# Retention followed by a squared-ReLU feed-forward: Strassen in eight groups for the first product, a scaled cast, a plain eviction and a new order

## The chip, the cores and the metric

The kernel runs on one core of a Trainium2 chip. The metric is the device time of one execution in microseconds (us). All inputs lie in the chip's memory in fp32, the output goes back there in fp32; in between the kernel works in fp16 with fp32 sums.

## The reference

```python
# q, k, v: [8 batch, 8 heads, 576 positions, 64]
scores = (q @ k^T) / sqrt(64)
ret    = scores * Dmat            # Dmat[h,i,j] = gamma_h ** (i-j) for i >= j, else 0
x      = (ret @ v) -> [4608 tokens, 512]        # heads side by side
h      = x @ w_in                               # w_in [512, 2048]
g      = relu(h) ** 2
out    = g @ w_out                              # w_out [2048, 512], out [4608, 512]
```

There are 4608 tokens. Most of the multiplications lie in the two products with `w_in` and `w_out`; the rest is the retention (a linear attention whose mask decays by a factor gamma to the distance, one gamma for each head).

## The kernel before

**Units and groups.** The 4608 tokens are cut into 36 units of 128 tokens. Of these, 32 are "full" units (128 positions of one batch) and 4 are "tails" (the last 64 positions of two batches). Two units make a group; there are 18 groups. The weights stay in SBUF as fp16, and a group passes through two stages.

**Retention of a group** (`add_casts`, `add_ret`). SyncE's queue loads q, k and v of a unit (256 KB each, L438 to L444). GpSimd casts them: k by a copy (L516), q by a copy (L527), v by a multiplication with a decay vector (L532). The cast k and q of the first eight units are transposed by TensorE (L584); for the other 28 units a DMA transposes them (tile `kqT`, L543). TensorE then works in small multiplications of 64x64 (all at L502): `psc` are the scores, `psS` the state of k and v that the next position block needs, `psO` the result. VectorE multiplies the scores by the mask (L838, tile `rT`), makes the decayed state (`Rm` L859, `stmp` L863, `R` L611) and multiplies the result by gamma to the position on the way out of PSUM (L898, tile `xT`). These 64x64 multiplications stand in dense blocks: the `psO` and `psc` of several units one after another. `PADS` (L202) says how many empty instructions the recorder sets between other multiplications ahead of each block.

**Feed-forward of a group** (`add_ff`). First product: for each pair of 128 columns of `w_in`, 4 multiplications of 128x256 for each half (L1229) fill a PSUM bank `ph`; ScalarE takes the relu into a tile `rl` (L1237), and ScalarE (L1247) or VectorE (L1249) squares it into `gT`. That is 64 multiplications of 128x256 for a group. Second product: group 0 in the plain way (L1270, 128x512), groups 1 to 17 by Strassen's method in the form of Winograd (`add_strassen`, L1327): seven products of half the size in each dimension instead of eight, from sums that VectorE makes (L1300, tile `gS`), and joined behind TensorE by copies on ScalarE (L1340) and additions on VectorE (L1350).

**Strassen for the first product** (`add_ff1s`) is used in groups 14, 15 and 16 (`FSET`). VectorE makes four small differences of `xT` (L1057). Each half j of the output columns takes seven products of 8 multiplications of 128x128 (L1072), so a group takes 112 of them. ScalarE copies three of the seven out of PSUM (L1085), VectorE adds two such parts and takes the relu (L1106), ScalarE takes the plain relu of one (L1100) and squares 1024 columns at a time (L1120). The four sums of weights that this needs (L1032, tile `wS`) are made by VectorE once; they wait for `xT` of groups 4 and on.

**What sets the order.** Every instruction is added to a recorder with an engine, dependences and the buffers that it takes and gives back. A planner (`emit`, L107) simulates the engines with fixed durations and takes the ready task with the lowest key; the keys stand in a list of 1794 numbers, `PLACES` (L20). Instructions are then issued in the order of that simulation, and each engine works in its own order, waiting on semaphores. In `add_ff1s` and `add_strassen` each product also depends on the one before it in the same group. The weights come in eight transfers of 512 KB on GpSimd's DMA queue (L478): four for `w_in`, then four for `w_out`.

Of the kernel before, what the change touches and what calls it, by code (L numbers as in the profile page):

```python
# [16 lines left out]
RESERVE_FROM = 200.0  # L17


PLACES = """  # L20
# [55 lines left out]
""".split()  # L76


# [1392 lines left out]
```

## Time and profile before

| what | value |
|---|---|
| runs (3) | 284.87, 284.90, 284.92 us; median 284.9 |
| span of the profiled execution | 284.5 us |
| lies around the span, against the median | 0.4 us |
| TensorE granted clock | full speed in every slice |
| TensorE busy | 277.1 us in 4490 instructions |
| VectorE busy | 195.8 us in 371 instructions |
| ScalarE busy | 190.6 us in 360 instructions |
| GpSimd busy | 87.3 us in 123 instructions |
| DMA | 50.0 MB, mean 176 GB/s |
| L1229, first product, plain | 960 multiplications of 128x256, 117.4 us busy |
| L1072, first product, Strassen | 336 multiplications of 128x128 |
| L898, `xT` out of PSUM | 28 of 683 ns on VectorE |
| L527, q's cast | 24 of 700 ns in the mean, on GpSimd |

Busy time is the time in which an engine's records cover the span. A multiplication's record is longer than its share of TensorE's time, since records overlap: a 128x256 record is 273 ns, but 40 of them take 4.37 us. So the cost of a multiplication is read from start to start in a run of equal ones, and not from the record. "DVE" is VectorE, "ACT" ScalarE, "POOL" GpSimd, "SP" SyncE, "PE" TensorE. A row of waits says which instruction waited, for whom, for how long in total, how often, and the longest.

### The profile page before, as it was taken

To read this page: it belongs to the slowest core of one execution; us is meant where nothing else is said; L and a number is where in the kernel's file an instruction comes from. 1 tells how busy PE (TensorE), PEld (TensorE's weight loads), DVE (VectorE), ACT (ScalarE), POOL (GpSimd) and SP (SyncE) were. 2 spreads that over 40 slices of the span, in tenths; PEclk is the share of its full clock that TensorE was granted. 3 is DMA by queue.
4 is the path that set the end of the run, shared out by engine and by line. 5 is a ranking of instruction groups with operands and counts; after the bars stand their busy time and mean duration, and the time that the engine had idled before them with its cause. 6 is when DMAs were issued, how large, how long until landed. Compare 5 with 4: busy or idle time off the path is not lost.

```text
span 284.5 us, 10916 instructions
## 1 busy us (share of the span) xinstructions
PE 277.1 (97%) x4490; PEld 237.7 (84%) x4490; DVE 195.8 (69%) x371; ACT 190.6 (67%) x360; POOL 87.3 (31%) x123
## 2 busy tenths in 40 slices
PE   8899999999999999899999999999999999999994
PEld 3578767888888888788888888888988999899883
DVE  4783489756867769635859485866986889765742
ACT  5659884678495848566575767577657486668830
POOL 6550035445334346434342523353243200000000
PEclk9999999999999999999999999999999999999999
DMA  7999998999997989999989969999998902020205
GB/s 204 291 207 205 261 313 233 155 241 167 197 189 165 225 193 177 195 241 198 234 196 215 208 163 198 200 146 249 200 168 215 193 0 78 2 76 1 76 0 150
DMA packets 119152, 50.00 MB, mean 176 GB/s; under 512 B 94784, under 2 KB 113728, under 8 KB 119104
## 3 DMA queue, kind: packets, MB, share of 16 engines
q1 hardware_dynamic: 114560, 44.84, 73.4%
q0 software_dynamic: 4224, 4.19, 8.9%
q8 instruction: 37, 0.61, 0.9%
q10 hardware_dynamic: 320, 0.26, 0.3%
q14 instruction: 11, 0.09, 0.1%
HBM read 36.70 MB, written 9.44 MB: 162 GB/s over the span
## 4 chain that ended last, share of the span: by engine, by line
PE 84%; DMA 11%; SPq 3%; POOL 1%; issue 0%; DVE 0%; POOLq 0%
PE po L1327 36%; PE ph L1229 31%; PE ph L1072 7%; DMA w_out<-in_moe_w_out_dram 6%; PE psO L502 4%; DMA pair<-in_v_dram 2%; PE po L1270 2%; PE psc L502 2%; PE psS L502 2%; DMA kqT<-kq 2%; SPq L460 1%; DMA loads<-in_v_dram 1%; SPq L463 1%; PE psT L584 1%; POOL w_out L478 1%; SPq L543 0%
## 5 line engine op out<-in xcount | busy, mean ns | idle before, releaser
L1229 PE MATMUL ph<-xT,w_in 128*128 128x256 f16 x960 | 117.4, 273 | 0.0
L1229 PEld LDWEIGHTS <-w_in 128*128 128x128 f16 x960 | 93.3, 98 | 11.8
L1237 ACT ACTIVATE rl<-ph 128x512 f16<-128x512 f32 x120 | 70.4, 590 | 42.3 <-PE ph L1229 41.7
L1247 ACT ACTIVATE gT<-rl 128x512 f16<-128x512 f16 x101 | 63.4, 630 | 2.7
L1327 PEld LDWEIGHTS <-gS 128*128 128x128 f16 x544 | 51.6, 98 | 6.1
L1327 PE MATMUL po<-wT,gS 128*128 128x256 f16 x408 | 54.9, 273 | 0.0
L1327 PEld LDWEIGHTS <-gT 128*128 128x128 f16 x408 | 39.5, 98 | 4.8
L1300 DVE TENSOR_TENSOR gS<-gT,gS 128x512 f16<-128x512 f16 (+1 forms) x51 | 32.3, 640 | 9.9 <-ACT gT L1247 9.2
L532 POOL TENSOR_TENSOR v<-loads,vdec_full 128x512 f16<-128x512 f32 x24 | 27.2, 1133 | 36.1 <-DMA loads<-in_v_dram 33.0
L1327 PE MATMUL po<-w_out,gT 128*128 128x256 f16 x272 | 37.6, 273 | 0.0
L1300 DVE TENSOR_TENSOR gS<-gT 128x1024 f16<-128x1024 f16 x34 | 25.7, 760 | 11.8 <-ACT gT L1247 9.0
L516 POOL CAST kq<-loads 128x512 f16<-128x512 f32 x32 | 22.1, 692 | 34.7 <-DMA loads<-in_k_dram 26.9
L1350 DVE TENSOR_TENSOR o<-po,u 128x256 f32<-128x256 f32 x33 | 13.9, 422 | 22.7 <-PE po L1327 14.6
L527 POOL CAST kq<-loads 128x512 f16<-128x512 f32 x24 | 16.8, 700 | 31.0 <-DMA loads<-in_q_dram 31.0
L1340 ACT COPY u<-po 128x256 f32<-128x256 f32 x34 | 12.4, 368 | 16.6 <-PE po L1327 16.4
L898 DVE TENSOR_TENSOR xT<-psO,gam_full 128x512 f16<-128x512 f32 x28 | 18.6, 683 | 5.8 <-PE psO L502 5.7
L1327 PE MATMUL po<-wT,gT 128*128 128x256 f16 x136 | 18.8, 273 | 0.0
L1327 PE MATMUL po<-w_out,gS 128*128 128x256 f16 x136 | 18.6, 273 | 0.0
L838 DVE TENSOR_TENSOR rT<-psc,mask_full 128x512 f16<-128x512 f32 x24 | 15.7, 681 | 0.6 <-PE psc L502 0.6
L1106 DVE CUSTOM_DVE_ANT_0 gT<-ph,loads 128x512 f16<-128x512 f32 x18 | 12.1, 685 | 4.2 <-PE ph L1072 3.5
L611 DVE TENSOR_TENSOR R<-stmp,dec 128x512 f16<-128x512 f32 (+1 forms) x18 | 13.5, 750 | 0.4
L1350 DVE TENSOR_TENSOR o<-po,p 128x256 f32<-128x256 f32 x18 | 7.6, 422 | 7.2 <-issue 3.5
(101 smaller groups left out, 310.3 us busy)
## 6 DMA issues: line engine op xcount, KB each, us to landing
out_dram<-o SPq DMA_DIRECT2D x32, 256.0 KB, 2.8
loads<-in_k_dram SPq DMA_DIRECT2D x24, 256.0 KB, 4.6
loads<-in_q_dram SPq DMA_DIRECT2D x96, 64.0 KB, 3.1
loads<-in_v_dram SPq DMA_DIRECT2D x24, 256.0 KB, 3.8
w_in<-in_moe_w_in_dram POOLq DMA_DIRECT2D x4, 512.0 KB, 8.9
w_out<-in_moe_w_out_dram POOLq DMA_DIRECT2D x4, 512.0 KB, 14.4
pair_c<-in_k_dram SPq DMA_DIRECT2D x2, 512.0 KB
pair_c<-in_q_dram SPq DMA_DIRECT2D x4, 256.0 KB
```

The costliest lines, as they stand in the source:

```text
L502: t = nc.tensor.matmul(out_, lhsT=lhsT, rhs=rhs, start=start, stop=True, skip_group_check=True, tile_position=(64 * row, 64 * col))
L516: op(out=out_.rearrange("p (n b a d) -> p n b a d", n=2, b=2, a=2), in_=in_.rearrange("p (a n b) d -> p n b a d", n=2, a=2))
L527: nc.gpsimd.tensor_copy(out=tile_of["kq", u][:, 1].rearrange("p (t a d) -> p a t d", t=4, a=2), in_=tile_of["q32", u].rearrange("p (a t) d ...
L532: nc.gpsimd.tensor_tensor(out=t, in0=tile_of["v32", u], in1=vdec[kind].rearrange("p (h o) -> p h o", o=1).to_broadcast([P, H, D]), op=ALU. ...
L898: nc.vector.tensor_tensor(out=tile_of["x", g].rearrange("p n (s e i) -> p e (n s) i", s=n, e=2)[:, c], in0=y.rearrange("p (o t r) -> p o r ...
L1072: nc.tensor.matmul(out_[:, e], lhsT=left[:, m, fi * P:(fi + 1) * P], rhs=right()[:, m], start=fresh and e == 0 and m == 0, stop=m == HK - ...
L1229: nc.tensor.matmul(tile_of["ph", g, fb][:, j, :], lhsT=w_in16[:, m, fi * P:(fi + 1) * P], rhs=tile_of["x", g][:, m, :], start=(m == 0), st ...
L1237: nc.scalar.activation(out=t, in_=tile_of["ph", g, fb], func=ACTF.Relu)
L1247: nc.scalar.activation(out=t, in_=rl, func=ACTF.Square)
L1300: (nc.gpsimd if eng == "POOL" else nc.vector).tensor_tensor(out=tile_of["S", g][:, k, sl], in0=in0(sl), in1=in1(sl), op=op)
L1327: nc.tensor.matmul(tile_of["pb", g, bank], lhsT=left(i), rhs=right[:, i, :], start=(start and i == 0), stop=(i == HF - 1), skip_group_chec ...
L1350: nc.vector.tensor_tensor(out=o_tile(u)[:, half * HM:(half + 1) * HM], in0=bank(x), in1=tile_of[name, g], op=ALU.add)
```

## The change

1. `FSET` goes from groups (14, 15, 16) to (4, 6, 8, 10, 12, 14, 15, 16): five more groups take the first product by Strassen.
2. q's cast on GpSimd becomes a multiplication by gamma to the position (`qdec`, made once at the start), so the result of the retention needs no such factor, and `xT` leaves PSUM by plain copies on ScalarE (`X_ENG`) instead of VectorE's multiplication.
3. The relu of a plain group writes `gT` at once and the square works in place; the pool of `rl` is gone.
4. The pool of Strassen's sums is replaced by fixed places: three sums for each parity of the group, the fourth written over a part of `gT`; copies of `add_ff1s` and the differences of `xT` have fixed places of their own.
5. In `add_ff1s` and `add_strassen` a product depends on the one before it in its own PSUM bank, not on the one before it in the group.
6. The sums of weights wait for no `xT`.
7. The planner is replaced by a written list, `ORDER`, of all tasks, and `PADS` is changed (417 empty instructions become 373).

Instructions after, by line of the changed kernel: 640 multiplications of 128x256 at L1163 (L1229 before), 896 of 128x128 at L1014 (L1072 before); the second product and the 64x64 multiplications keep their numbers.

```diff
-    FSET = (14, 15, 16)
-    BOTH = (14, 15, 16)
+    FSET = (4, 6, 8, 10, 12, 14, 15, 16)
+    BOTH = (4, 6, 8, 10, 12, 14, 15, 16)
+    X_ENG = ("ACT", "ACT")
-    PADS = (136, 0, 0, 0, 121, 0, 84, 0, 76, 0, 0, 0, 0)
+    PADS = (121, 0, 0, 0, 68, 0, 0, 0, 0, 0, 0, 125, 59)
...
     def emit(self):
-        for t, x in zip(self.tasks, PLACES):
-            t["key"] = int(x)
...
+        order = [self.tasks[int(x)] for x in ORDER]
...
+    gS_at = [flat_stage[:, y, 0:1536].bitcast(FP16).rearrange("p (s f t) -> p s f t", s=3, t=P) for y in range(2)]
+    part_at = {"p1q": flat_stage[:, 0, 1536:2048], "u2q": flat_stage[:, 1, 1536:2048], "u4q": parts}
+    xs_at = const.tile([P, 3, NP // 2, P], FP16, name="xs")
...
         def fq():
...
-                nc.gpsimd.tensor_copy(out=tile_of["kq", u][:, 1].rearrange("p (t a d) -> p a t d", t=4, a=2),
-                                      in_=tile_of["q32", u].rearrange("p (a t) d -> p a t d", a=2))
+                nc.gpsimd.tensor_tensor(out=out_.rearrange("p (t a d) -> p a t d", t=4, a=2),
+                                        in0=tile_of["q32", u].rearrange("p (a t) d -> p a t d", a=2),
+                                        in1=by.rearrange("p (a t o) -> p a t o", a=2, o=1).to_broadcast([P, 2, 4, D]), op=ALU.mult)
...
-                nc.vector.tensor_tensor(
-                    out=tile_of["x", g].rearrange("p n (s e i) -> p e (n s) i", s=n, e=2)[:, c],
-                    in0=y..., in1=gam_f[...], op=ALU.mult)
+                (nc.scalar.copy if X_ENG[c] == "ACT" else nc.vector.tensor_copy)(
+                    out=tile_of["x", g].rearrange("p n (s e r t) -> p e (n s) r t", s=n, e=2, t=4)[:, c],
+                    in_=y...)
...
-            p6 = product(j, 6, "a", wS[1], T2, [t[2], c1, p7], False, at(2))
+            p6 = product(j, 6, "a", wS[1], T2, [t[2], c1], False, at(2))
-            p5 = product(j, 5, "a", wS[0], T1, [t[0], c2, p2], False, at(4))
+            p5 = product(j, 5, "a", wS[0], T1, [t[0], c2], False, at(4))
-            p4 = product(j, 4, "c", wA[1, 1], T4, [t[3], r22, p3], False, at(6))
+            p4 = product(j, 4, "c", wA[1, 1], T4, [t[3], r22], False, at(6))
...
             def fr(fb=fb):
-                t = tile_of["rl", g, fb] = r_pool.tile([P, nf, n * P], FP16, name="rl", tag="rl")
-                nc.scalar.activation(out=t, in_=tile_of["ph", g, fb], func=ACTF.Relu)
+                nc.scalar.activation(out=tile_of["g", g][:, nf * fb:nf * (fb + 1), :], in_=tile_of["ph", g, fb], func=ACTF.Relu)
...
-                    nc.scalar.activation(out=t, in_=rl, func=ACTF.Square)
+                    nc.scalar.activation(out=t, in_=t, func=ACTF.Square)
```

Where the prediction speaks of the changed kernel it uses that kernel's lines: L1163 and L1014 (first product, plain and Strassen), L1201 (plain second product), L1256 (Strassen's second product), L470 (q's cast), L784 (`rT`), L803 and L805 (`Rm`), L555 (`R`), L845 (`xT` on ScalarE), L999 (differences of `xT`), L1023 (copies), L1042 (addition with relu), L1056 (squares of 1024 columns), L1229 (sums `gS`), L1271 and L1281 (copies and additions of the second product).

More of the change, by code (lines that the diff above doesn't have):

```diff
@@ L107, in emit @@
     def emit(self):
-        assert len(PLACES) == len(self.tasks)
-        for t, x in zip(self.tasks, PLACES):
-            t["key"] = int(x)
-        ready = {e: [] for e in self.LAT}
-        busy = {e: False for e in self.LAT}
-        events = []
-        order = []
-        seq = 0
-        def push(at, what, t):
-            nonlocal seq
-            seq += 1
-            heapq.heappush(events, (at, seq, what, t))
-        for t in self.tasks:
-            if t["left"] == 0:
-                heapq.heappush(ready[t["eng"]], (t["key"], t["n"], t))
@@ L194, in emit @@
-        assert len(order) == len(self.tasks)
+        order = [self.tasks[int(x)] for x in ORDER]
+        assert len(order) == len(self.tasks) == len(set(ORDER))
+        for t in order:
+            assert t["left"] == 0, t["n"]
+            for w in t["users"]:
+                w["left"] -= 1
         self.place_runs([t for t in order if t["eng"] == "PE"])
@@ L216, in place_runs @@
         between = []
-        for t in tasks:
+        for i, t in enumerate(tasks):
             if t["size"] > 190:
@@ L220, in place_runs @@
                 between = []
-            elif t["size"] <= 8 and t["key"] < 10 ** 6 and t["start"] > 24.0:
+            elif t["size"] <= 8 and i >= self.FIRST_PAD:
                 between.append(t)
@@ L671, in add_ret_pair @@
             if s or carry:
-                chain.append(add("DVE", base + 5.5 + s, 0.42, fr1(s), deps=[t] + (chain[-1:] if s else [T["R", g - 1]])))
+                chain.append(add("DVE", base + 5.5 + s, 0.42, fr1(s), deps=[t] + (chain[-1:] if s else [T["R", g - 1]]), acq=("stmp",)))
                 if not s:
@@ L1033, in add_wS @@
                 ts.append(add("DVE", WS_KEY + 2 * i + h, 0.66, f,
-                              deps=[d[h] for d in deps] + T["kvx", 4] + T["qx", 4] + [T["x", groups[WS_GROUP + 2 * i + h][0]]] + sum((wcast[x] for x in range(4)), []), soft=True))
+                              deps=[d[h] for d in deps] + T["kvx", 4] + T["qx", 4] + sum((wcast[x] for x in range(4)), []), soft=True))
             return ts
@@ L1079, in copy_to @@
         def copy_to(name, j, key, deps):
-            n = PARTS_OF.index(name)
-            at = (NU - PAIRED + (2 if n else 3) * FSET.index(g) + j + (not n)) % LD
             def f():
-                t = tile_of[name, g, j] = loads[:, (3 * at + n) * H * D:(3 * at + n + 1) * H * D]
-                nc.scalar.copy(out=t, in_=bank(j, "a").rearrange("p e t -> p (e t)"))
-            t = add("ACT", key, 0.6, f, deps=deps + holders[n, at], acq=("ld" + "kqv"[n],))
-            holders[n, at] = held[name, j] = []
-            return t
+                nc.scalar.copy(out=part_at[name], in_=bank(j, "a").rearrange("p e t -> p (e t)"))
+            return add("ACT", key, 0.6, f, deps=deps + T["kvx", 6] + T["qx", 6] + T["kvx", 2], acq=(name,))
         def g_at(s, h, j):
@@ L1328, in f @@
                                          start=(start and i == 0), stop=(i == HF - 1), skip_group_check=not start)
-                last[:] = [add("PE", at_(key + q), 0.2184, f,
-                               deps=last + deps(q // 2) + (reads if q == 0 else []) + wT_done.get(k, []),
-                               acq=("ff",) + more if start and q == 0 else (), size=4, inside=k > 1)]
-            return last[0]
+                chain[bank] = [add("PE", at_(key + q), 0.2184, f,
+                                   deps=chain.get(bank, []) + deps(q // 2) + (reads if q == 0 else []) + wT_done.get(k, []),
+                                   acq=("ff",) + more if start and q == 0 else (), size=4, inside=k > 1)]
+                if k == 1 and q == 0:
+                    T["ff2first"] = chain[bank][:]
+            return chain[bank][0]
         raw = lambda s, i: (lambda f: tile_of["g", g][:, i * HF + f, s * P:(s + 1) * P])
-        summed = lambda k: (lambda f: tile_of["S", g][:, k, f, :])
+        summed = lambda k: (lambda f: gS_at[g % 2][:, k - 1, f, :] if k else raw(1, 0)(f))
         bank = lambda x: tile_of["pb", g, x]
@@ L1354, in add_strassen @@
         if g == last_g:
-            last[:] = []
+            chain.clear()
             at = -2 * NF * n
@@ L1424 @@
     for g in range(len(groups)):
+        sched.at = ("casts", g)
         add_casts(g)
     for g in range(len(groups)):
+        sched.at = ("ret", g)
         add_ret(g)
+    sched.at = None
     for u in range(NU):
@@ L1433 @@
             sched.free("R", T["Rread", g])
-    for u in range(NU - LD, NU):
-        for n in range(3):
-            holders[n, (u - PAIRED) % LD] = T["casts", u]
     make_wS()
     for g in range(len(groups)):
+        sched.at = ("ff", g)
         add_ff(g)
```

186 lines of the change are left out of this document (66 added, 120 removed), and 110 rows, old and new, of tables (ORDER, PLACES).

## The prediction

> **What bounds the kernel now.** I read the page's busy times and slices first, then the chain that ended last.
>
> ```profile
> PE 277.1 (97%) x4490; PEld 237.7 (84%) x4490; DVE 195.8 (69%) x371; ACT 190.6 (67%) x360; POOL 87.3 (31%) x123
> PE   8899999999999999899999999999999999999994
> PEclk9999999999999999999999999999999999999999
> PE 84%; DMA 11%; SPq 3%; POOL 1%; issue 0%; DVE 0%; POOLq 0%
> ```
>
> TensorE is full from the second slice to the last but one, at full clock, and holds 84% of the chain; the DMA's 11% lies at the start and at one place behind it, and no other compute engine has over 1%. So TensorE's own work sets the time, and whatever makes it wait is added. Its price is read from runs of equal multiplications in the chain:
>
> ```profile
> 138.94 4.37 PE ph L1229 x40
> ...
> 225.03 3.57 PE ph L1072 x64
> ```
>
> That is 4.37/40 = 109.2 ns for one 128x256 and 3.57/64 = 55.8 ns for one 128x128. Next come the view of waits and the timeline of TensorE, for what interrupts it:
>
> ```profile
> PE psc L502 <- DMA kqT<-kq: 1.1, 1, 1.1
> ...
> PEld L502 <- DMA kqT<-kq: 1.2, 1, 1.2
> ```
>
> ```profile
> 23.83 3.44 PE L1229 MATMUL ph<-xT,w_in 128*128 128x256 f16 x30
> 27.10 1.03 PE L1270 MATMUL po<-w_out,gT 128*128 128x512 f16 x4
> 27.97 1.91 PE L1229 MATMUL ph<-xT,w_in 128*128 128x256 f16 x16
> 29.71 1.03 PE L1270 MATMUL po<-w_out,gT 128*128 128x512 f16 x4
> 30.58 1.91 PE L1229 MATMUL ph<-xT,w_in 128*128 128x256 f16 x16
> 32.54 1.02 PE L1270 MATMUL po<-w_out,gT 128*128 128x512 f16 x4
> ```
>
> One wait of 1.25 us, start to start, lies at 115 us: a block of scores stands before its transposed k and q have landed. At the start the four quarters of `w_out` are met just as they land (26.66, 29.20, 32.50 and 35.05 us by the trace), and only the third costs anything (0.22 us). Two smaller waits of 0.2 and 0.15 us lie at 208.6 and 244 us.
>
> **The terms.** All against the span of 284.5 us; the runs' median is 0.4 us above it, which I add at the end.
>
> *Strassen in five more groups.* Each loses 64 x 109.2 ns = 6.99 us and gains 112 x 55.9 ns = 6.26 us. By the totals: 320 x 109.2 ns against 560 x 55.9 ns gives **-3.5 us**. All of it is on TensorE, so all counts if nothing else gets late.
>
> *ScalarE and VectorE, busy time.* ScalarE gets two `xT` copies for each of the later groups (like L1237's 590 ns) and 29 more copies, loses relus and squares; I sum the rows to 206 us of 284. VectorE loses L898's 28 and gains 30 additions like L1106 and 20 differences of 288 ns: 200 to 204 us. Neither becomes the bound by its total. So the question is where one is late.
>
> ```profile
> L898 DVE TENSOR_TENSOR xT<-psO,gam_full 128x512 f16<-128x512 f32 x28 | 18.6, 683 | 5.8 <-PE psO L502 5.7
> L1106 DVE CUSTOM_DVE_ANT_0 gT<-ph,loads 128x512 f16<-128x512 f32 x18 | 12.1, 685 | 4.2 <-PE ph L1072 3.5
> ```
>
> *Copies in a Strassen bank.* Between a product and its successor in the same bank stand six multiplications in the new order (0.654 us; eight, 0.874 us, before). The cover needed is 0.201 us (a multiplication's turn over to ScalarE's start), 0.366 (copy) and 0.053 (release to TensorE): 0.62. Some 20 places are left with only 0.05 us or so. I cost them at nothing; each would cost what its copy starts late, as when another ScalarE instruction (590 ns) stands before it.
>
> *VectorE behind blocks.* I walked VectorE's and ScalarE's queues of the changed order between the multiplication that feeds them and the one that needs their result, row by row, with instructions overlapping by 82 ns as independent ones do in the trace. Before, no such place is late. After, four are, all behind a dense block of 64x64 work. The nearest to read, nominally at 223.4 us: L1042 0.681, L1281 0.42, L999 0.287, L555 0.69, L784 0.681, L999 twice 0.287, L784 0.681 sum to 4.01 us; less 7 x 0.082, plus 0.201 and 0.053, gives 3.70 us. TensorE meanwhile has 12 128x256 (1.31), a block of 96 small ones (0.93 and 0.09 for entering it), 8 of 128x128 (0.45) and 2 more 128x256 (0.22): 3.0 us. So 0.7 us late. The others give 0.87 (172.6), 0.40 (131.5) and 0.37 us (214.5). Bounds: nothing, if I misjudge what hangs on which, and 3.5 us, if each queue also starts late. I take the walk, **+2.3 us**, since its durations vary by under 3%.
>
> *The start.* The new order puts the first multiplication with `w_out` (L1201) four multiplications behind the first use of the last quarter of `w_in`, which landed at 24.15 us. It stands 2.6 us of work earlier than before: TensorE gets there at about 24.6 us, and the quarter lands at 26.66. The transfers are 2.5 us apart on busy DMA engines, and the change moves no weight transfer, so TensorE waits: **+2.0 us**. Bounds: 0, if the queue delivers sooner, and 2.6, if something ahead is later still (16 small memsets and five more iotas stand before the first work). Later quarters then have slack.
>
> *The wait at 115 us.* In the trace 19.14 MB of loads and transposes had been issued on SyncE's queue at 107.0 us and 20.19 MB, the transpose waited for, at 112.3; it landed 4.35 us later (chain), and its block was ready at 115.3. The new order's block there needs 19.40 MB, issued by the same rate at 108.3 and landed at 112.7; TensorE reaches it at about 113.8 (104.9 us of work, and 8.9 us behind its work since the start). So it goes, with 1.1 us to spare: **-1.25 us**; kept, if GpSimd's longer casts or the queue use that up. The small waits at 208.6 and 244 us go with the old order: -0.35 us.
>
> *q's multiplication on GpSimd.* 24 casts go from L527's row to L532's, without gain or loss on TensorE if GpSimd's idle time (69%) hides it:
>
> ```profile
> L532 POOL TENSOR_TENSOR v<-loads,vdec_full 128x512 f16<-128x512 f32 x24 | 27.2, 1133 | 36.1 <-DMA loads<-in_v_dram 33.0
> ...
> L527 POOL CAST kq<-loads 128x512 f16<-128x512 f32 x24 | 16.8, 700 | 31.0 <-DMA loads<-in_q_dram 31.0
> ```
>
> That is 24 x 0.43 us and the tails, 10 to 12 us on an engine at 87. GpSimd waits 31 us for q alone, so it keeps up. The transposes start 0.4 us later; they land some us ahead of use. Cost 0 on this path, but see rival C.
>
> *Places, relu in place, dependences by bank, empty instructions.* They cost nothing by themselves: multiplications keep 109.2 ns with 0 to 4 empty instructions between them. Their effect is the order, which the terms above take from the new lists.
>
> Sum: -3.5 + 2.3 + 2.0 - 1.25 - 0.35 = -0.8. Span 283.7, **284.1 us** as runs go.
>
> **Rivals.**
>
> *A, VectorE keeps up.* The four late places cost nothing. For it: margins there rest on many small latencies. Against: the rows are steady. -3.5 + 2.0 - 1.25 - 0.35 = -3.1: 281.8 us.
>
> *B, it nets out.* The DMA wait stays in another place, since kqT then still competes with 50 MB at 73% of 16 engines' time. -3.5 + 2.3 + 2.0 - 0.35 = +0.4: 285.3 us.
>
> *C, GpSimd holds VectorE (slower).* VectorE's operations with both inputs in SBUF stretch beside GpSimd, and those that read PSUM do not:
>
> ```profile
> 93.19 0.68 DVE L1300 TENSOR_TENSOR gS<-gT 128x1024 f16<-128x1024 f16 x1
> 93.79 1.53 DVE L1300 TENSOR_TENSOR gS<-gT,gS 128x1024 f16<-128x1024 f16 x1
> ```
>
> ```profile
> 93.58 1.20 POOL L532 TENSOR_TENSOR v<-loads,vdec_full 128x512 f16<-128x512 f32 x1 [1.04 <-DMA loads<-in_v_dram]
> ```
>
> A sum of 0.68 us takes 1.53 beside v's multiplication: +0.85. Beside q's copies the excess stayed at 0.1 to 0.4; with multiplications it would be 0.85 as well. Half the small sums already show some (mean 527 ns, shortest 411). The place is the queue behind a block, where nothing is left over; it decides from the second such hit on (0.8 us of gain plus the bound below). Three of the four late places hit: 3 x 0.85 = +2.5, so 286.6 us; all four 287.5. The Trainium skill ("SBUF — State Buffer", section "Who interferes with whom") says that a VectorE instruction with two SBUF inputs contends with a GpSimd one that reads SBUF, and that who comes second is blocked for the whole; the row above agrees.
>
> *D, weight loads bound the small multiplications.* Each 128x128 needs a load of its own, and a load's record is longer than the multiplication's turn:
>
> ```profile
> L1229 PEld LDWEIGHTS <-w_in 128*128 128x128 f16 x960 | 93.3, 98 | 11.8
> ```
>
> Were 98 ns the floor, 560 of them would take 54.9 us and not 31.3: +23.6, so 308 us. Against it stand 336 in the trace at 55.8 ns, load and all; loads overlap. The Trainium skill ("TensorE: Matmul & The Clock Gate", section "Back-to-back issue gap") gives about 81 ns for a sustained stream of 128 columns with loads; by that an estimate would be +14 us, and the change could only lose. The trace differs from it.
>
> **How the numbers follow.** A difference of 0.2%, 0.57 us, is about what a measurement of this kernel can tell from no change: 284.3 to 285.5 is "same". Forecast (282.8 to 284.8 by its terms) 0.37, of it 0.30 faster and 0.07 same. A 0.22, all faster. B 0.18, of it 0.15 same and 0.03 slower. C 0.22, slower. D 0.01, slower. So faster 0.52, same 0.22, slower 0.26. The range leaves out half of A's lower side and the upper third of C: **281.6 to 286.8**.
>
> **What would show it.** L1163 640 times at 109 ns and L1014 896 times at 56 ns start to start: the first term. A wait of TensorE for a DMA of `w_out` between 24.5 and 26.7 us: the second. Waits of TensorE for `rT` L784 or `xT` after blocks near 131, 173, 214 and 223 us: the third; if instead VectorE idles there, rival A. A row "psc <- DMA kqT": B. L470 above 1.0 us and L1229's means well above 527, 760 and 865 ns: C. I am wrong if a new wait on ScalarE's copies appears (the 0.05 us margins), which I cost at nothing: 20 of them at 0.1 us would take 2 us.

## The result and the profile after

The changed kernel takes 292.38 us in the median of its runs (291.17 to 298.25) against 284.88 before: ratio 1.0254 (1.0218 to 1.0289), **slower by 2.5%**. The forecast was 284.1 us, and the range ended at 286.8. Medians here are over all runs of a kernel, ratios over the undisturbed ones, so the two can differ (by 1.5% in experiment 6).

First the page of the changed kernel: busy times, TensorE's slices, and the chain's shares.

```profile
span 291.3 us, 11387 instructions
PE 276.6 (95%) x4730; PEld 236.9 (81%) x4730; DVE 200.8 (69%) x405; ACT 199.7 (69%) x374; POOL 101.1 (35%) x133
PE   7997999999999999999999999999979999999993
PE 64%; DMA 11%; DVE 11%; SPq 6%; issue 3%; ACT 2%; POOL 1%; DVEq 0%; POOLq 0%
```

TensorE holds 64% of the chain, against 84% in the profile predicted from and 95% in the second one of before; VectorE has 11% where it had none. That second profile was taken of the kernel before as it is (experiment 5):

```profile
span 283.1 us, 10916 instructions
PE 276.1 (98%) x4490; PEld 237.2 (84%) x4490; DVE 196.5 (69%) x371; ACT 190.7 (67%) x360; POOL 86.4 (31%) x123
PE   7899999999999999999999999999999999999994
PE 95%; POOL 2%; issue 2%; DVE 0%; POOLq 0%
```

This execution is 1.4 us shorter than the one predicted from, and TensorE waits for nothing at 115 us in it. All runs here lie 1.7 us above their own span, this one too (284.88 for 283.1). So I estimate that the execution predicted from itself took about 286.2 us: 1.3 us off the median, and the wait of 1.25 us at 115 us, which the second profile lacks, accounts for it.

Busy time hides the loss (TensorE's is nearly the same), so I split each span at TensorE, from its records. *Work* is the sum of the turns of all multiplications, start to start, each by its shape, with what entering and leaving a block of small ones adds; *head* is what TensorE took beyond its turns in the first 11.5 us of work; *late* is what it falls behind its turns from there to the start of its last multiplication; *end* is the rest. The small multiplications have no single turn, so some 0.5 us can be moved between work and late, in all rows alike. In us:

| kernel | head | work | late | end | span |
|---|---|---|---|---|---|
| before, predicted from | 5.10 | 270.83 | 4.62 | 3.96 | 284.5 |
| before, again | 5.09 | 270.83 | 2.93 | 4.23 | 283.1 |
| changed | 5.01 | 267.49 | 13.46 | 5.31 | 291.3 |

The work did fall, by 3.34 us: 320 x 109.2 ns less 560 x 55.8 ns is 3.7, and the new order cuts the small multiplications into 28 blocks instead of 26, each with some 0.2 us for entering and leaving (the turn ahead of a block takes 203 ns instead of 109.2, the last one in it 118 to 148). Against the second execution of before, late grew by 10.5 and the end by 1.1. The view of waits and the timeline of TensorE tell where. The waits of the changed kernel, longest first (in total, times, longest):

```profile
PE po L1201 <- DMA w_out<-in_moe_w_out_dram: 1.9, 1, 1.9
PE ph L1163 <- issue: 1.8, 1, 1.8
...
PE psc L441 <- DMA kqT<-kq: 0.6, 2, 0.5
PE ph L1014 <- DVE rT L784: 0.6, 2, 0.4
```

Its timeline (start, length, engine, line) at the start and at 217 us:

```profile
23.25 1.92 PE L1163 MATMUL ph<-xT,w_in 128*128 128x256 f16 x16
...
27.11 0.38 PE L1201 MATMUL po<-w_out,gT 128*128 128x512 f16 x1 [1.94 <-DMA w_out<-in_moe_w_out_dram]
```

```profile
214.67 0.27 PE L1163 MATMUL ph<-xT,w_in 128*128 128x256 f16 x1
...
216.77 0.97 PE L1163 MATMUL ph<-xT,w_in 128*128 128x256 f16 x7 [1.82 <-issue]
```

Measured start to start, the 13.46 us of this profile are: the wait for `w_out` 2.1; a wait of 2.0 at 216.8 us that nothing in the profile explains ("issue"); two waits for transposes, 0.35 at 105 and 0.66 at 127 us; ten places behind VectorE, 4.7 in all; and 3.7 in small pieces, where before has 2.9 in all.

The prices of the multiplications are what they were. The chain of the changed kernel has

```profile
146.15 1.34 PE ph L1014 x24
...
241.47 1.95 PE ph L1014 x32
```

55.8 and 61 ns each, the second with a 0.2 us wait within.

### The profile page after: what moved, and what is told of

The parts are those of the page before. It is cut to its first block, busy times and chain, and to the rows that moved or that the text cites. A ratio compares the mean times of both kernels' runs of the same rounds, so it can differ in the third digit from the quotient of the medians.

```text
span 291.3 us, 11387 instructions
## 1 busy us (share of the span) xinstructions
PE 276.6 (95%) x4730; PEld 236.9 (81%) x4730; DVE 200.8 (69%) x405; ACT 199.7 (69%) x374; POOL 101.1 (35%) x133
## 4 chain that ended last, share of the span: by engine, by line
PE 64%; DMA 11%; DVE 11%; SPq 6%; issue 3%; ACT 2%; POOL 1%; DVEq 0%; POOLq 0%
PE po L1256 27%; PE ph L1163 18%; PE ph L1014 13%; DMA w_out<-in_moe_w_out_dram 4%; DMA kqT<-kq 2%; PE psO L441 2%; PE po L1201 2%; DMA stage<-in_v_dram 2%; DVE stage L1229 2%; DVE rT L784 2%; DMA loads<-in_v_dram 1%; SPq L399 1%; DMA out_dram<-o 1%; SPq L377 1%; DVE gT L1229 1%
## 5 line engine op out<-in xcount | busy, mean ns | idle before, releaser
L1163 PE MATMUL ph<-xT,w_in 128*128 128x256 f16 x640 | 84.4, 273 | 2.0 <-issue 1.8
L1163 PEld LDWEIGHTS <-w_in 128*128 128x128 f16 x640 | 61.1, 98 | 11.4 <-issue 2.5
L1172 ACT ACTIVATE gT<-ph 128x512 f16<-128x512 f32 x80 | 46.8, 596 | 25.3 <-PE ph L1163 25.3
L1256 PEld LDWEIGHTS <-gT 128*128 128x128 f16 x544 | 50.7, 98 | 7.6 <-issue 1.5
L1256 PE MATMUL po<-w_out,gT 128*128 128x256 f16 x272 | 45.1, 273 | 0.3 <-DVE rT L784 0.3
L1256 PE MATMUL po<-wT,gT 128*128 128x256 f16 x272 | 42.1, 273 | 0.3 <-DVE o L1281 0.3
L1256 PE MATMUL po<-wT,stage 128*128 128x256 f16 x272 | 41.8, 273 | 0.1
L1256 PEld LDWEIGHTS <-stage 128*128 128x128 f16 x408 | 37.7, 98 | 5.1 <-DVE stage L1229 0.4
L1179 ACT ACTIVATE gT<-gT 128x512 f16<-128x512 f16 x66 | 39.6, 629 | 0.3
L1042 DVE CUSTOM_DVE_ANT_0 gT<-ph,stage 128x512 f16<-128x512 f32 x32 | 22.0, 687 | 19.4 <-PE ph L1014 14.3
L1014 PEld LDWEIGHTS <-pair_c 128*128 128x128 f16 x512 | 33.0, 98 | 2.5 <-issue 1.1
L1056 ACT ACTIVATE gT<-gT 128x1024 f16<-128x1024 f16 x32 | 33.2, 1056 | 1.3 <-DVE gT L1042 1.0
L470 POOL TENSOR_TENSOR kq<-loads,qexp 128x512 f16<-128x512 f32 x24 | 26.5, 1104 | 19.5 <-DMA loads<-in_q_dram 18.1
L1229 DVE TENSOR_TENSOR stage<-gT,stage 128x512 f16<-128x512 f16 (+1 forms) x51 | 31.6, 626 | 0.6
L1023 ACT COPY stage<-ph 128x512 f32<-128x512 f32 x32 | 18.7, 587 | 11.7 <-PE ph L1014 9.9
L1014 PEld LDWEIGHTS <-w_in 128*128 128x128 f16 x384 | 24.8, 98 | 2.2 <-issue 1.0
L1281 DVE TENSOR_TENSOR o<-po,u 128x256 f32<-128x256 f32 x33 | 13.8, 421 | 17.9 <-ACT u L1271 10.9
L1271 ACT COPY u<-po 128x256 f32<-128x256 f32 x34 | 12.7, 373 | 15.6 <-PE po L1256 15.6
L1256 PE MATMUL po<-w_out,stage 128*128 128x256 f16 x136 | 22.6, 273 | 0.0
L845 ACT CAST xT<-psO 128x512 f16<-128x512 f32 x28 | 15.7, 589 | 7.8 <-PE psO L441 7.5
```

What stands on the lines that cost most here:

```text
L470: nc.gpsimd.tensor_tensor(out=out_.rearrange("p (t a d) -> p a t d", t=4, a=2), in0=tile_of["q32", u].rearrange("p (a t) d -> p a t d", a= ...
L1014: nc.tensor.matmul(out_[:, e], lhsT=left[:, m, fi * P:(fi + 1) * P], rhs=right()[:, m], start=fresh and e == 0 and m == 0, stop=m == HK - ...
L1023: nc.scalar.copy(out=part_at[name], in_=bank(j, "a").rearrange("p e t -> p (e t)"))
L1042: nc.vector._custom_dve(TENSOR_ADD_SAT, out=g_at(s, h, j), in0=bank(j, x), in1=part_at[name].rearrange("p (e t) -> p e t", t=P), s0=3.4028 ...
L1056: nc.scalar.activation(out=t, in_=t, func=ACTF.Square)
L1163: nc.tensor.matmul(tile_of["ph", g, fb][:, j, :], lhsT=w_in16[:, m, fi * P:(fi + 1) * P], rhs=tile_of["x", g][:, m, :], start=(m == 0), st ...
```

## The experiments

Three theories stood at the start. **W**: the loss is a list of separate waits (`w_out`, 217 us, end), each to be undone by its own edit. **V**: it is mainly VectorE behind blocks, as the sums come ahead of the reads of PSUM that TensorE waits for. **C**: those places are late since GpSimd's multiplication of q holds VectorE. In the experiments' kernels L1011, L1160, L1226 and L1253 are what the page after has at L1014, L1163, L1229 and L1256, and so on.

**1. The changed kernel again**, without an edit.

> The changed kernel as it is, a second profile of it. Theory: the 1.8 us in which TensorE waits for nothing visible at 215 us is a late fetch of its instructions, which depends on the moment, so it is gone or elsewhere in this profile, and a span without it is about 289.3 us; the waits on VectorE behind the blocks (4 to 5 us together), on the transposes (1.0 us) and on the first quarter of w_out (2.1 us) stand at the same places within 0.1 us. Rival: the 1.8 us belongs to the place (the order and the number of empty instructions set where the code runs dry), so it stands at 215 us again.

293.96 us (292.37 to 297.71), ratio 1.0300 (1.0275 to 1.0325). Late 14.4 for 13.5. The "issue" wait stands at the same place in the list, with 0.8 us; in the eight profiles whose list is unchanged there it took 0.4 to 2.0. So it belongs to the place. The other waits do not hold still as I expected: those for transposes are gone, so the 1.0 us of the first profile was an accident of it, and the places behind VectorE cost more. Adding up all places over 0.09 us where VectorE released TensorE, start to start, gives 8.2 us for 4.4 in the first profile. The largest is the place at 231 us, 1.6 us for 0.2:

```profile
PE ph L1011 <- DVE Rm L802: 1.4, 1, 1.4
```

Just ahead of it two VectorE instructions with both inputs in SBUF take 1.23 and 0.92 us instead of 0.41 each, beside GpSimd's multiplication of v, which in the first profile came later. So what VectorE costs differs from execution to execution. The ratios of these two sets of runs of one kernel lie 1.3 us apart, so gains are given against both below.

**2. GpSimd copies q** again, as before the change (the factor left out).

```diff
-  nc.gpsimd.tensor_tensor(out=..., in0=tile_of["q32", u]..., in1=by..., op=ALU.mult)
+  nc.gpsimd.tensor_copy(out=..., in_=tile_of["q32", u]...)
```

> GpSimd casts q by a copy as before instead of multiplying; the factor gamma to the position is left out of the result. Theory that GpSimd's longer work holds VectorE's sums and delays the transposes: GpSimd's busy time falls by 10 to 11 us, the mean of VectorE's small sums falls toward 500 ns, TensorE's waits on VectorE behind blocks and on transposes fall from about 5.7 to about 4 us, time 1.5 to 2 us less than the changed kernel's. Rival, the order of VectorE's queue alone makes them: the waits stay within 0.4 us of 5.7 and the time within 0.5 us.

290.12 us, ratio 1.0204 (1.0162 to 1.0245): by ratios 2.7 us below experiment 1 and 1.4 below the changed kernel's first runs, by medians 3.8 and 2.3. Late fell from 14.4 to 10.3, and the places behind VectorE from 8.2 (4.4 in the first profile) to 2.8. VectorE's groups with both inputs in SBUF, multiplying (first fence) and copying (second), in busy time and mean ns:

```profile
L1226 DVE TENSOR_TENSOR stage<-gT,stage 128x512 f16<-128x512 f16 x34 | 17.5, 525 | 0.4
...
L552 DVE TENSOR_TENSOR R<-stmp,dec 128x512 f16<-128x512 f32 x12 | 11.6, 964 | 0.0
...
L996 DVE TENSOR_TENSOR xs<-xT,xs 128x256 f16<-128x256 f16 x16 | 6.3, 392 | 0.0
```

```profile
L1222 DVE TENSOR_TENSOR stage<-gT,stage 128x512 f16<-128x512 f16 x34 | 16.2, 486 | 0.4
...
L548 DVE TENSOR_TENSOR R<-stmp,dec 128x512 f16<-128x512 f32 x12 | 9.5, 794 | 0.0
...
L992 DVE TENSOR_TENSOR xs<-xT,xs 128x256 f16<-128x256 f16 x16 | 4.5, 281 | 0.0
```

Theory C holds: no instruction of VectorE was edited, and three of its groups got shorter by 7 to 28%. That the transposes now start earlier can't be the reason, since experiment 1 has no wait for one either. The size stays rough: against the first runs the intervals of the ratios overlap. Experiment 13 repeats the edit.

**3. First use of `w_out` later**: in the list, six tasks of the second product of group 0 go some places further back.

```diff
- ... 53 533 508 ... 54 534 552 ... 553 515 556 ... 501 516 559 ... 557 517 66 ... 567 518 58 ...
+ ... 560 533 534 557 ... 564 515 516 554 ... 568 517 518 513 ...
```

> The first seven multiplications tasks with w_out stand behind 2.6 us more of the first product. Theory that the wait of 2.1 us for the first quarter of w_out is a loss of its own: the wait goes, time 1.5 to 2.1 us less than the changed kernel's. Rival, given back: later stretches wait for the loads and VectorE anyway (TensorE only comes earlier to the waits at 52, 81, 105 and 127 us), so under 0.7 us of it reach the end.

292.18 us, ratio 1.0249 (1.0214 to 1.0283): by ratios 1.5 us below experiment 1, but only 0.1 below the first runs, so no gain is shown. The wait is gone, but much of its 1.9 us comes back: from 11.5 to 40 us of work late fell from 2.90 to 1.41 us, from 40 to 60 it rose from 1.31 to 2.67, where TensorE now meets GpSimd's work on q and v for the first units. TensorE arriving earlier finds others late.

**4. Group 16 ends ahead of group 17**: the tails of the two groups no longer alternate.

```diff
- ... 1742 1728 1833 1811 1743 1812 1802 1749 1750 1813 ...
+ ... 1742 1728 1743 1802 1749 1750 1746 ... 1764 1766 1765 1833 1811 1812 1813 ...
```

> At the end all of group 16's second product stands ahead of group 17's instead of between its parts, so that its two stores of 256 KB leave some 3 us earlier. Theory that the end costs 1.1 us more than before because four transfers are issued one after another behind the last addition: from TensorE's last multiplication to the end of the span it takes about 4 us instead of 5.0, time 0.8 to 1.3 us less than the changed kernel's. Rival: the alternation covers the turn-over from bank to bank, and without it TensorE waits for copies by as much, so no change within 0.4 us.

294.36 us, ratio 1.0299 (1.0259 to 1.0339): no gain. The end fell from 5.32 to 4.64 us, but in this order TensorE waits 0.62, 0.62, 0.41 and 0.19 us for copies between the last products. Why the changed kernel's end is long is seen on SyncE's queue, where its last five stores are issued one behind another:

```profile
285.18 0.55 SPq L962 DMA_DIRECT2D out_dram<-o  x1
285.82 0.75 SPq L957 DMA_DIRECT2D out_dram<-o  x1
286.66 2.12 SPq L962 DMA_DIRECT2D out_dram<-o  x3
```

Before, four remain:

```profile
277.94 0.39 SPq L1011 DMA_DIRECT2D out_dram<-o  x1
278.42 1.80 SPq L1016 DMA_DIRECT2D out_dram<-o  x3
```

From VectorE's last addition to the end of the span it is 3.5 us there, and 4.6 in the changed kernel.

**5. The kernel before, again**, to have a second profile of it.

> The kernel before as it is, a second profile of it. The prediction's span of 284.5 us stood 0.4 us under the median of the runs, while later runs lie 1.7 us above their own spans. Theory: the profiled execution that the prediction was made from was itself some 1.3 us slower than the median, because the wait of 1.25 us for a transpose at 115 us is an accident of that execution; here the span is 282.5 to 283.5 us and that wait is absent or below 0.3 us. Rival: the wait belongs to the order, and stands at 115 us again.

284.8 us, ratio 1.0004 (0.9985 to 1.0022). TensorE's waits in it:

```profile
PE warm L411 <- DVE wT L292: 1.3, 1, 1.3
PE psc L502 <- DVE kqT L601: 0.6, 1, 0.6
PE psS L502 <- POOL vx L562: 0.3, 1, 0.3
```

No wait for a DMA at 115 us: that one was an accident of the execution predicted from. A loss of 0.28 us at 243.3 us, in the first profile at 245.0, stands here too; the changed kernel has it as well.

**6. Empty instructions ahead of two blocks**, to move the wait at 217 us. TensorE's code comes in by its instruction queue in pieces of 16 KB (38 transfers, 0.62 MB); with the 256 empty instructions more of this experiment it is 39, so a piece holds 256 instructions. The dense block at 211.7 us is 128 small multiplications, over 256 instructions with their loads, which TensorE takes in 1.25 us; counted from the first record, it starts at 0.54 of a piece. Of the other blocks of 96 and more, one of 112 starts there too, without a wait; the rest lie lower, at 0.18 to 0.43. The fetch of a piece began at 214.2 us, 2.6 behind the block's start, and took 1.07; TensorE stood from 214.9 to 216.8. So the theory is that TensorE ran out of code.

```diff
-    PADS = (121, 0, 0, 0, 68, 0, 0, 0, 0, 0, 0, 125, 59)
+    PADS = (121, 0, 0, 0, 68, 0, 0, 0, 0, 128, 128, 125, 59)
```

> The changed kernel with 128 empty instructions more ahead of each of two dense blocks, the one at about 212 us and the next, and none else moved. Theory: the wait of 0.8 to 2.0 us behind the block at 212 us is TensorE running out of fetched instructions at that place of the code; with the code shifted by 128 instructions it is gone (under 0.2 us), and the time 0.8 to 2.0 us less than the changed kernel's. Rival: the block simply outruns the fetch wherever the boundary lies, so the wait stays over 0.8 us.

295.95 us, ratio 1.0254 (1.0236 to 1.0272). The edit was a bad one: the block at 212 us moved by 256 instructions, a whole piece, so it stands where it stood, and its wait stayed, with 0.48 us. But the block of 112 ahead of it, moved by half a piece to 0.03, now has a wait of 0.40 us within it that it had in no profile before.

**7. The scaling undone**: GpSimd copies q, and VectorE multiplies by gamma on the way out of PSUM as before; all else as in the changed kernel.

```diff
-    X_ENG = ("ACT", "ACT")
+    X_ENG = ("DVE", "DVE")
...
-                (nc.scalar.copy ...)(out=tile_of["x", g]..., in_=y...)
+                nc.vector.tensor_tensor(out=tile_of["x", g]..., in0=y..., in1=gam_f..., op=ALU.mult)
```

> The part with q undone, in the changed kernel's order: q cast by a copy on GpSimd, xT multiplied by gamma on VectorE on the way out of PSUM. VectorE gets 19 us more, ScalarE 16 us less, GpSimd 10 us less. Theory that GpSimd's longer multiplications cost the changed kernel 3 to 4 us: they go, but 28 operations of 683 ns come into VectorE's queue, two behind every block, so that its late places grow by up to 0.7 us each: time within 1.5 us of the changed kernel's, on either side. Rival, VectorE's queue behind blocks has slack for them: 3 to 4 us less, about 290 us, as with the copy alone.

297.0 us, ratio 1.0438 (1.0422 to 1.0454), late 17.6: worse than the changed kernel by 3.0 us against experiment 1 and 4.6 against its first runs, and neither expectation had it. The places behind VectorE cost 10.5 us. These 28 instructions are back in VectorE's queue behind the blocks:

```profile
L838 DVE TENSOR_TENSOR xT<-psO,gam_full 128x512 f16<-128x512 f32 x28 | 19.1, 683 | 6.8 <-PE psO L438 6.6
```

So under this order the move of `xT` to ScalarE saves more than q's multiplication costs: VectorE, though busy for 69%, is what TensorE waits for behind blocks.

**8. VectorE reads PSUM first**: at four blocks its masks (`rT`) and state reads (`Rm`) go ahead of the sums for the next product. One of the four, with 1265 a sum:

```diff
- ... 1315 1316 1265 1319 1317 1320 440 1310 262 1323 436 438 ...
+ ... 1315 1316 440 1319 1317 1320 436 1310 262 1323 1265 438 ...
```

> Behind four blocks (at about 141, 184, 230 and 240 us) VectorE's reads of PSUM (rT, Rm) stand ahead of its sums and squares; nothing else is moved. Theory that these places are late by the order of VectorE's queue: the waits there, about 3 us together, fall under 1 us, and the time is 1.5 to 2.5 us less than the changed kernel's. Rival: the sums that now come later make TensorE wait as long, so no change within 0.5 us.

290.3 us, ratio 1.0203 (1.017 to 1.0235): by ratios 2.8 us below experiment 1 and 1.5 below the first runs, where the intervals overlap, by medians 3.7 and 2.1. Theory V holds: in its profile the places behind VectorE cost 2.9 us, and late is 11.35 for 14.4, though a halved clock (last section) takes 1.7 of that. VectorE in the changed kernel at 140 us, with GpSimd and then TensorE at the same time:

```profile
139.75 0.75 DVE L1229 TENSOR_TENSOR stage<-gT,stage 128x512 f16<-128x512 f16 x2
140.42 1.53 DVE L1229 TENSOR_TENSOR gT<-gT 128x1024 f16<-128x1024 f16 x1
141.87 0.68 DVE L784 TENSOR_TENSOR rT<-psc,mask_full 128x512 f16<-128x512 f32 x1
142.47 0.67 DVE L805 TENSOR_TENSOR Rm<-psS,R 128x512 f16<-128x512 f32 x1
143.07 0.67 DVE L784 TENSOR_TENSOR rT<-psc,mask_full 128x512 f16<-128x512 f32 x1
```

```profile
140.23 1.17 POOL L470 TENSOR_TENSOR kq<-loads,qexp 128x512 f16<-128x512 f32 x1 [2.32 <-DMA loads<-in_q_dram]
```

```profile
142.60 0.38 PE L1256 MATMUL po<-w_out,gT 128*128 128x256 f16 x2 [0.28 <-DVE rT L784]
143.20 0.61 PE L1014 MATMUL ph<-xT,w_in 128*128 128x128 f16 x8 [0.22 <-DVE Rm L805]
```

The sum takes 1.53 us beside q's multiplication (L470) instead of 0.68, the mask behind it is late by that much, and TensorE waits for the mask. In experiment 8 the masks come first, and the same sum starts 0.1 us ahead of a cast of GpSimd and takes 0.67:

```profile
142.86 0.68 DVE L781 TENSOR_TENSOR rT<-psc,mask_full 128x512 f16<-128x512 f32 x1
143.46 0.67 DVE L802 TENSOR_TENSOR Rm<-psS,R 128x512 f16<-128x512 f32 x1
144.06 0.67 DVE L781 TENSOR_TENSOR rT<-psc,mask_full 128x512 f16<-128x512 f32 x1
144.66 0.67 DVE L1226 TENSOR_TENSOR gT<-gT 128x1024 f16<-128x1024 f16 x1
```

```profile
144.77 1.03 POOL L452 CAST kq<-loads 128x512 f16<-128x512 f32 x1 [2.78 <-DMA loads<-in_k_dram]
```

Now it is the cast that is long: k's cast took 0.61 us at 144.23 in the changed kernel. Who comes second pays. Instructions that read one input from PSUM stay near 0.67 us in both.

**9. Other empty instructions**, chosen so that the block at 212 us starts at 0.20 of a piece instead of 0.54.

```diff
-    PADS = (121, 0, 0, 0, 68, 0, 0, 0, 0, 0, 0, 125, 59)
+    PADS = (121, 0, 0, 0, 68, 0, 0, 0, 0, 0, 168, 213, 59)
```

> The changed kernel with 168 empty instructions more ahead of the block at 212 us and 88 more ahead of the next, so that the block at 212 us begins at 0.20 of a piece of 256 instructions instead of 0.54 and all other blocks stay where they were. (In the run before this one, the block at 212 us was moved by 128 + 128, a whole piece, so its place in the piece had not changed.) Theory: TensorE's code is fetched in pieces of 256 instructions some 3 to 4 us after the need shows, and a block of 258 instructions that begins late in a piece leaves too few behind it; with 0.20 the wait behind the block is gone (under 0.2 us) and the time 0.8 to 2.0 us less than the changed kernel's 293.5. Rival: it stays over 0.4 us at that place.

297.74 us, ratio 1.0452 (1.0407 to 1.0497). The wait behind the block is gone, but 0.5 us (start to start) now stand within it, again without a releaser (first row), and the time is worse: the recorder puts up to nine empty instructions between two multiplications, and there they are not free (second row).

```profile
219.31 0.26 PE L438 MATMUL psS<-v,kq 64*64 64x64 f16 x8 [0.34 <-issue]
...
219.94 2.68 PE L1253 MATMUL po<-w_out,gT 128*128 128x256 f16 x16
```

That is 16 multiplications in 2.68 us, where 16 x 109.2 ns is 1.75. The prediction had up to four as free. In the profile no two empty instructions start less than 70 ns apart, and from 219.94 to 225.45 us there are 70 of them, so they alone take 4.9 us, beside multiplications worth 3.4.

**10. Experiments 3, 8 and 9 together** (their three edits).

> Three orders mended together in the changed kernel: VectorE's reads of PSUM first behind four blocks, the first multiplications with w_out later, the block at 212 us moved within its piece of code. Theory that the causes add: 290.3 less 1.5 to 2.1 (w_out) less 0.8 to 1.5 (code), about 287.3 us. Rival, what is taken away comes back at the next place: over 289 us.

293.87 us, ratio 1.0303 (1.0266 to 1.0339): the empty instructions eat the gain of the other two, and the block at 213 us has 0.87 us without a releaser within it.

**11. Experiment 10 with three more tasks of VectorE moved, and group 16's stores on GpSimd's queue.**

```diff
- ... 1494 ... 1502 1493 ...
+ ... 1493 ... 1502 1494 ...
...
- ...store(u, o_tile(u))...
+ ...store(u, o_tile(u), engs=late)...
```

> The same three, and four more: three places where a VectorE result that TensorE waits for moves ahead of a sum that is wanted later (at 85, 112 and 233 us), and the two stores of group 16 go through GpSimd's queue, which is idle at the end, instead of SyncE's. Theory: 0.3 to 0.9 us less at each of the three places, 0.5 to 0.9 us less at the end (the last addition to the end of the span 3.8 us instead of 4.6); together 2 us less than the three alone, about 285.3 us. If all the found causes are the whole of the loss, this comes within 1 us of the kernel before, and not far below it. Rival: places that are not found yet take it up, over 287 us.

293.57 us, ratio 1.0307 (1.0279 to 1.0334), the same as 10. The end is not shorter (5.63 us for 5.33): in this profile GpSimd's queue is no faster way for these stores.

**12. All that helped**: the blocks of 8 and two more, the moved tasks of 11, the edit of 3, stores as they were, and 51 empty instructions fewer at one place, so that the block at 212 us starts elsewhere in a piece.

```diff
-    PADS = (121, 0, 0, 0, 68, 0, 0, 0, 0, 0, 0, 125, 59)
+    PADS = (121, 0, 0, 0, 17, 0, 0, 0, 0, 0, 0, 125, 59)
```

> All found orders mended in the changed kernel: VectorE's reads of PSUM first behind six blocks, three sums moved, the first multiplications with w_out later, stores as they were, and the code shifted by 51 empty instructions fewer ahead of the fifth block (17 for 68) instead of 256 more, so that the block at 212 us begins at 0.34 of a piece. Theory that the last two kernels were slow by their empty instructions (up to nine between two multiplications, 5 us together) and otherwise as hoped: 285.5 to 287 us, no waits without a releaser over 0.4 us behind the block at 212 us. If so, the changed kernel's loss is its order and what GpSimd does to it, and the 3.5 us of Strassen come back only in part, because the tail (1.3 us) and small waits stay. Rival: there is a loss that none of these reach, over 288 us.

289.91 us, ratio 1.0184 (1.0147 to 1.022). Late 9.6 us, no wait behind the block at 212 us, which now starts at 0.34 of a piece. It is still 5.1 us above before by medians. What is left is spread over many places (behind VectorE 3.3 us), the first five of its waits, without the 1.3 us at the start that every profile has:

```profile
PE psO L438 <- issue: 1.1, 2, 0.7
PE po L1253 <- DVE stage L1226: 0.7, 1, 0.7
PE ph L1011 <- DVE gT L1039: 0.6, 1, 0.6
PE psS L438 <- POOL vx L503: 0.6, 1, 0.6
PE ph L1011 <- DVE xs L996: 0.6, 2, 0.4
```

The first row is the wait for code again: two other blocks, which the same edit moved to 0.98 and 1.00 of a piece, now lose 0.90 and 0.55 us within them. The wait was moved and not removed.

**13. Experiment 12 with q copied** (the factor left out; the edit of experiment 2).

> The same, with q cast by a copy on GpSimd; the factor gamma to the position is left out of the result. In the changed kernel's own order the copy gave 3.4 us. Theory that GpSimd's longer multiplications hurt through VectorE's late places: where these have slack again the copy gives less, 0.5 to 1.5 us. Rival, they hurt everywhere alike (the ports, the later transposes): 3 us or more again, which would be below the kernel before.

287.35 us, ratio 1.0112 (1.0082 to 1.0142), late 7.1: q's multiplication costs 2.0 (ratios) to 2.6 us (medians) even in a mended order, and the places behind VectorE fall from 3.3 to 0.7 us. In both profiles of before there is none. Against the second profile of before, the 1.8 us that remain in the span are late +4.2, end +1.1, work -3.3 and head -0.1. No version made here beats the kernel before. Of the 4.2, the two waits for code have 1.3 (0.62 and 0.66 us); the rest was not tried further.

## Why the prediction was wrong

**Right.** Strassen on TensorE: -3.34 us for -3.5, with 55.8 ns for 128 columns (the sum's own prices, 320 x 109.2 ns less 560 x 55.9, give 3.6; the two blocks more, which I did not count, take 0.4 back). The Trainium skill ("TensorE: Matmul & The Clock Gate", section "Back-to-back issue gap") has about 81 ns there; 560 more of them at 55.8 ns disagree again, and rival D falls. The wait for `w_out`: 2.1 us for 2.0, though experiment 3 shows that taking it away need not give it back at the end. The copies in Strassen banks: none of TensorE's eleven longest waits in either profile of the changed kernel is for ScalarE, so the thin margins of 0.05 us held.

**The credit for waits that go (-1.6 us) was wrong.** The wait at 115 us was an accident of one execution, as experiment 5 shows. Of the two small ones, the one at 244 us stands in all four profiles of the two kernels, so nothing was to be gained there; the one at 208.6 us is gone in experiment 5. The hint was there: I read "0.4 us around the span" as a property of the runs, while all other runs have 1.7. The changed kernel's 1.0 us for transposes at 105 and 127 us is of the same kind: its second profile has none.

**q's multiplication on GpSimd, costed at 0, was the step that failed in kind.** The mechanism stood in the text as rival C, with 0.85 us for a hit, and the trace shows just that hit at 140 us. But I set it beside the forecast as a chance where it had to be a term: 24 multiplications spread over four fifths of the span can meet many queues, and not three. Undoing it alone gave 1.4 to 3.8 us (experiment 2, by the runs it is set against), and 2.0 to 2.6 in the mended order (experiment 13). The Trainium skill ("SBUF — State Buffer", section "Who interferes with whom") has the rule, that the second of the two is blocked; the runs agree, in that sums of 0.68 us go to 1.53 behind a multiplication of GpSimd, a cast of 0.61 goes to 1.03 behind a sum, and reads of PSUM do not move. Rival C's own 286.6 us was too low as well, for the next reasons.

**VectorE behind blocks, costed at 2.3 us, was sized wrong: 4.7 us in the first profile, and far more in the second** (8.2 for 4.4 by places over 0.09 us). In the first, the four places that I named cost 3.0, most of the excess in the one at 131.5 us (0.97 near 143 us in the trace, for 0.40). Six more that I had not found cost 1.7. The walk took durations without GpSimd, and it took sums in the order of the list as given; experiment 8 shows by 1.5 to 2.8 us that this order is a cause of its own. Nor is the term one number: which sums meet GpSimd changes with the execution. Part of these 4.7 us and of q's price are the same time, so the two must not be added.

**Not counted at all:** the fetch of code at the dense block (2.0 us in the first profile; 0.4 to 1.6 in others with the same list there) and the end, longer by 1.1 us since two groups finish together and SyncE issues five stores in a row.

The first profile of the changed kernel against the second of before: forecast without the credit for waits, -0.8 + 1.6 = +0.8 us; measured +8.2. The difference of 7.4 is VectorE 2.4, code 2.0, end 1.1, transposes 1.0, work 0.2, `w_out` 0.1, and some 0.7 in small pieces, less 0.1 at the head.

## What to carry to other kernels

Compare a profiled execution's span with the median before you credit a change with a wait that goes; a wait that a second profile doesn't have is worth nothing. Profile the changed kernel twice as well: here its waits on VectorE were 4.4 us in one execution and 8.2 in the next. When a change adds GpSimd instructions that read SBUF, treat their contact with VectorE's two-input sums as a term of the sum, for every queue that ends in something TensorE waits for. An order that puts sums ahead of the reads that free PSUM turns each stretched sum into a stall, and the saved multiplications are soon spent: here 3.3 us of work went against 10.5 us of lateness. Empty instructions that move code past a wait move the wait too, so look at all blocks behind them.

## What the runs showed of the hardware

**The clock halved behind gaps of 2.30 and 2.48 us.** The view by stretches of experiment 8 gives, for 28.4 to 31.6 us, the length, busy time and count of PE, PEld, DVE, ACT and POOL, then the granted clock, the DMA share and GB/s:

```profile
28.40:31.60 3.20, 3.20 (x16) 2.06 (x15) 0.00 (x0) 1.10 (x3) 0.00 (x0) 0.50 1.24 206
```

Sixteen multiplications take what some thirty would. Ahead of it TensorE had stood for 2.30 us, start to start, until 27.6 us, and in experiment 6 for 2.48 us, until 190.3 us; each time the granted clock was 0.50 for 3.41 us, worth 1.7 us. Gaps of 1.9 to 2.27 us elsewhere, one of them in experiment 6 itself, had no such sequel. The Trainium skill ("TensorE: Matmul & The Clock Gate", section "🎯 Why this matters for your kernels") asks for no idle gap over some 3 us; in these runs the edge lies lower, near 2.3 us.

**A dense block can outrun the fetch of code, and the wait stands where a piece ends.** Number TensorE's records of a profile (multiplications, weight loads, empty instructions) from 0 and divide by 256: behind the first 17.7 us, all 15 profiles together have 24 places where TensorE lost over 0.38 us and no releaser is seen, and at all 24 the remainder is 193 or 194. So the wait belongs to the step from one piece of code to the next, wherever the edits put it (behind a block in the changed kernel, within blocks in experiments 6, 9 and 12). The times of the transfers say how. In the changed kernel TensorE passed such a place at 211.87 us, within the dense block; the transfer of the next piece started 2.34 us later and took 1.07; TensorE, which had stood since 214.9 us, went on at 216.77, 2.55 us behind the transfer's start. In none of the 15 profiles does TensorE enter a piece less than 2.2 us behind the start of its transfer, and over half of the transfers in each start over 1 us after the piece before was entered. Code that is used up faster than that waits: a block takes over 256 instructions in 1.25 us. The Trainium skill ("Runtime: NRT & Kernel Launch", section "Instruction fetch mechanics") has pieces of 256 instructions as well, and the crossing from one to the next mostly hidden; here most crossings cost nothing that can be seen, and those near dense blocks 0.4 to 2.0 us. What stays open is when a transfer starts: in the two profiles of the changed kernel the one at this place started 2.34 and 1.45 us after the piece before was entered, and the wait was 2.0 and 0.8 us.
